# Attention followed by a low-rank token mixer and an MLP: where the third batch's attention begins, when a group's norms are issued, and the place of four small pieces of preparation

## The chip, the cores and the metric

The kernel runs on one core of a Trainium2 chip. The metric is the device time of one execution in microseconds. Before the change the median of three runs is 596.51 us (595.23 to 598.22). One more execution was profiled: 596.88 us, of which 595.1 us lie between the program's first and last instruction (the span).

## The reference, cut to what matters

```python
q, k, v: (8, 12, 448, 64)        # batch, heads, tokens, head size
q_n, k_n = rmsnorm(q, g_q), rmsnorm(k, g_k)
attn = softmax(q_n @ k_n.T / 8)
x = (attn @ v)                   # as (8, 448, 768)
h = x.transpose(0, 2, 1) @ U @ V # mixing over the tokens, rank 32
u = x + h.transpose(0, 2, 1)
out = u + relu(u @ w_ch1) @ w_ch2   # 768 -> 3072 -> 768
```

## The kernel before, in words

**Groups.** The 12 heads of a batch are worked in three groups of four; groups are numbered through all batches (group 3 is the first of the second batch, b = 1; group 6 the first of the third, b = 2). A group has two pairs of heads; a pair is named (b, pr).

**A group's preparation.** `load` (L125) puts its q, k and v into a set of three fp32 tiles (three sets take turns) by six DMAs on SP's queue. `squares` (L133) multiplies q and k with themselves, on ScalarE or GpSimd. `sums` (L159) adds up the squares on VectorE. `scale_all` (L203) issues `roots` (two small ScalarE instructions, L163), the scaling of q and k by them on GpSimd (L171, or L179 from group `DMA_FROM` = 6 on) and `values`, GpSimd's copies of v in bf16 (L197). Groups 1 to 5 are then turned by TensorE (`turn`, L347) and taken to SBUF by VectorE (`take_q`, `take_k`). From group 6 on four DMA transposes on SP's queue turn them (`turn_dma`, L373) and GpSimd multiplies the turned q with the gains (`take_dma`, L381). The scaled q (`qn`) and k (`kp`) have one buffer each, the turned ones (`qT`, `kT`) two.

**A pair.** `Sc` (L401) makes scores of 128 keys for both heads in one of two PSUM buffers and ScalarE takes their exponentials (L414). The last keys of both heads share one short block (`sl`). `Srows` issues two or three such blocks. `V` (L423) multiplies the exponentials with the values for half of the tokens; VectorE divides by the sum (L442) and writes `x` (L443).

**A batch's rest.** `mix_t` and `mix_tr` (L453, L462) project `x` to rank 32 and turn the result; `mix_rows` (L499), eight times, adds the mixed part to `x` on VectorE, and for each block of tokens an SP transpose writes `uT` (L521). `up` (L541: 24 times, six products each) makes the hidden layer, with the relu on ScalarE or VectorE; `down` (24 or 32 parts of six products, L552) the output, which VectorE adds to `x` (L569) and SP stores (L577). Batch 0 takes its own path through its mixing, with `prep_u` (L323), two casts of U, and `prep_v`, GpSimd's copies of V to `Vm`.

**Order.** No scheduler moves anything: each engine executes in the order in which the Python code issues. What comes first is an order written by hand (L605 to L641, and the calls from L752 on: there the loads of group 3's q and k stand ahead of group 2's v). Then two lists are merged: `att`, the attention of batches 1 to 7 and what prepares it (L643 to L718), and `mlp` (L729 to L750). Each entry has a cost in us. The loop at L820 takes the next entry of `att` as long as the cost taken so far is not above `due(cm)`, where `cm` is the cost taken from `mlp`; else it takes from `mlp`, where a batch's entries may begin once its attention is issued. `due` (L806) rises in one line up to the end of batch 1's attention while batch 0's MLP list runs, and in a second line over all that is left. An entry of cost 0 is issued where it stands. `load` is put off while a batch's `mix_rows` are being issued (`later`). `weights(n)` issues the next n pieces of the two weight matrices on GpSimd's queue.

In the merged order of before, around the change (groups in brackets):

```
up(0,21)  sums[6]  scale_all[6]  up(0,22)  Srows(1,4: two blocks)  turn_dma[6]  load[7]  take_dma[6]
weights(2)  V(1,3) x2  up(0,23)  Srows(1,4 and 1,5)  down(0,64) x2  V(1,4)  ...  V(1,4)  down
squares[7] on ScalarE  sums[7]  load[8]  V(1,5)  down  V(1,5)  down  Srows(2,0)  down x3  mix_t(1) ...
scale_all[7]  load[9]  Srows(2,0 and 2,1)  mix_rows(1) with down  ...  turn_dma[7]  take_dma[7]
```

Of the kernel before, what the change touches and what calls it, by code (L numbers as in the profile page):

```python
# [18 lines left out]
ROWS_FROM = 1  # L19
DMA_FROM = 6  # L20
LEAD = 1.8


@with_exitstack
def kernel(
# [13 lines left out]
    nc = tc.nc  # L39
# [3 lines left out]
    rank = moe_U.shape[1]  # L43
# [9 lines left out]
    NW = len(WIN[0])  # L53
# [19 lines left out]
    groups = []  # L73
# [16 lines left out]
    def load_qk(gi, i, eng=None):  # L90
        b, h0, n = groups[gi]
        if gi == BESIDE:
            for a in range(2):
                nc.sync.dma_start(staged[gi][i][a * R:(a + 1) * R].rearrange("p (c j) d -> p c (j d)", c=2),
                                  (q, k)[i][b, h0 + 2 * a:h0 + 2 * a + 2].rearrange("c (p j) d -> p c (j d)", j=NT))
            return
        src = (q, k)[i][b, h0:h0 + n].rearrange("(c a) (p j) d -> (a p) c (j d)", a=2, j=NT)
        (eng or nc.sync).dma_start(staged[gi][i].rearrange("p (c j) d -> p c (j d)", c=2), src)
# [4 lines left out]
    def load_v(gi, eng=None):  # L103
        b, h0, n = groups[gi]
        t = staged[gi][2]
        toks = v[b, h0:h0 + n].rearrange("h (p j) d -> p h (j d)", j=NT)
        for i in range(2):
            (eng or nc.sync).dma_start(
                t[i * R:(i + 1) * R, :NM, :].rearrange("p (h j) d -> p h (j d)", j=NJ),
                toks[:, :, i * NJ * D:(i + 1) * NJ * D])  # L110
        for e in range(2):
            hs = slice(e, 4, 2) if gi == BESIDE else slice(2 * e, 2 * e + 2)
            (eng or nc.sync).dma_start(t[e * R:(e + 1) * R, NM:, :], toks[:, hs, 2 * NJ * D:])

    def stage_tiles(gi):
        staged[gi] = [stage.tile([P, NM + 2, D], FP32, name=nm, tag=nm) for nm in ("qf", "kf", "vf")]
        ssqs[gi] = normp.tile([P, 2, NM + 2], FP32, name="ssq", tag="ssq")
        normed[gi] = [normp.tile([P, NT, 2, D], BF16, name="qn", tag="qn", bufs=1)]
        if gi < DMA_FROM:
            normed[gi].append(kp[:, :NT].rearrange("p j (c d) -> p j c d", c=2))  # L120
        else:
            normed[gi].append(kp)
        normed[gi] += [va_bufs[gi % 3], vl_bufs[gi % 3]]
# [167 lines left out]
    Ub = consts.tile([P, NJ + 2, rank], BF16)  # L291
    first = xp.tile([P, NW, dm], BF16, name="x", tag="x")
    Uf = first[:, 2, :2 * (NJ + 2) * rank].bitcast(FP32).rearrange("p (j r) -> p j r", r=rank)
# [3 lines left out]
    def load_u():  # L297
        for i in range(2):
            nc.sync.dma_start(Uf[i * R:(i + 1) * R, :NJ, :], Urows[:, i * NJ:(i + 1) * NJ, :])
        nc.sync.dma_start(Uf[R:P, NJ, :], Urows[:, 2 * NJ, :])  # L300
        nc.sync.dma_start(Uf[0:R, NJ + 1, :], Urows[:, 2 * NJ, :])
        nc.sync.dma_start(Vf, moe_V.rearrange("(m r) s -> m r s", m=1).to_broadcast([NQ, rank, S]))
# [17 lines left out]
    Uz = first[:, 0, :NW * P].rearrange("p (j r) -> p j r", r=P)  # L320
    tz = first[:, 1, :]

    def prep_u():  # L323
        nc.vector.tensor_copy(Ub, Uf)
        nc.vector.tensor_copy(Uz[:, :, :rank], Uf[:, :NW, :])

    tb_bufs = [consts.tile([P, 2 * P], BF16, name=f"tb{i}") for i in range(2)]

# [252 lines left out]
    att = []  # L581

    def add_att(cost, f, *a):
        att.append((cost, f, a))
# [17 lines left out]
    def turns(gi):  # L602
# [12 lines left out]
        (2, 1): scales(2) + [(0, weights, (1,)), V2(1, 0)],  # L615
        (2, 2): [(0, keep_busy, (6,))],
        (2, 3): [V2(1, 1), (0, prep_u, ())],
        (3, 0): [(0, keep_busy, (6,))],
        (3, 1): [V2(2, 0)],
# [23 lines left out]
    for i, (b, pr) in enumerate(pairs):  # L643
        if b == 0:
            continue
        gi, a = divmod(i, 2)
        more = gi + 1 < len(groups)
        by_dma = gi + 1 >= DMA_FROM
        soon = gi + 2 < len(groups)

        if a == 0:
            if pr == 0 and b > 1:
                add_att(0.5, V, *pairs[i - 1], 0)
                add_att(0.5, V, *pairs[i - 1], 1)
            add_att(0.45, Srows, ((b, pr, 0), (b, pr, 1)))
            if gi + 1 == DMA_FROM:
                add_att(0.0, turn_dma, gi + 1)
                add_att(0.0, load, gi + 2)
                add_att(0.0, take_dma, gi + 1)
                add_att(0.0, weights, 2)  # L660
            elif gi == DMA_FROM:
                add_att(0.0, scale_all, gi + 1)
                add_att(0.0, load, gi + 3)
            elif by_dma and more:
                add_att(0.0, scale_all, gi + 1)
            if b == 1 and pr == 0:
                add_att(0.8, lambda: None)
            if not by_dma:
                add_att(0.0, squares, gi + 1, 0, nc.gpsimd)
                add_att(0.0, squares, gi + 1, 1, nc.gpsimd)  # L670
                if gi + 2 < DMA_FROM:
                    add_att(0.0, load, gi + 3)
            if pr != 0:
                add_att(0.4, V, *pairs[i - 1], 0)
                add_att(0.5, V, *pairs[i - 1], 1)
            if not by_dma:
                add_att(0.0, sums, gi + 1, 0)
                add_att(0.0, sums, gi + 1, 1)
            add_att(1.0, Srows, ((b, pr, 2), (b, pr + 1, 0), (b, pr, 3)))
            if more and gi + 1 > DMA_FROM:  # L680
                add_att(0.0, turn_dma, gi + 1)
                add_att(0.0, take_dma, gi + 1)
                if gi > DMA_FROM and gi + 3 < len(groups):
                    add_att(0.0, load, gi + 3)
            if not by_dma:
                add_att(0.0, scale_all, gi + 1)
                if gi + 2 >= DMA_FROM:
                    add_att(0.0, squares, gi + 2, 0, nc.gpsimd)
                    add_att(0.0, squares, gi + 2, 1, nc.gpsimd)
            add_att(0.4, V, b, pr, 0)  # L690
        else:
            add_att(0.6, Srows, ((b, pr, 1), (b, pr, 2), (b, pr, 3)))
            if not by_dma:
                add_att(0.5, V, *pairs[i - 1], 1)
                add_att(0.39, T, gi + 1, 0)
                add_att(0.39, T, gi + 1, 1)
                if gi + 2 == DMA_FROM:
                    add_att(0.0, sums, gi + 2, 0)
                    add_att(0.0, sums, gi + 2, 1)
                    add_att(0.0, scale_all, gi + 2)  # L700
                continue
            if gi + 1 == DMA_FROM:
                add_att(0.5, V, *pairs[i - 1], 1)
                add_att(0.0, squares, gi + 2, 0)
                add_att(0.0, squares, gi + 2, 1)
                add_att(0.0, sums, gi + 2, 0)
                add_att(0.0, sums, gi + 2, 1)
                add_att(0.0, load, gi + 3)
                continue
            if soon:  # L710
                add_att(0.0, squares, gi + 2, 0)
                add_att(0.0, squares, gi + 2, 1)
            add_att(0.5, V, *pairs[i - 1], 1)
            if soon:
                add_att(0.0, sums, gi + 2, 0)
                add_att(0.0, sums, gi + 2, 1)
# [4 lines left out]
    done_at = {}  # L721
# [63 lines left out]
    sums(2, 0)  # L785
    stage_tiles(3)
    load_u()
    load_qk(3, 0)
    load_qk(3, 1)
    load_v(2)  # L790
    load_v(3)

    ia = im = 0
# [1 line left out]
    a_from = done_at[0]  # L795
    a_all = sum(c for c, _, _ in att[a_from:])
    a_one = sum(c for c, _, _ in att[a_from:done_at[1]])
    m_all = sum(m[0] for m in mlp)
    m_one = 0.0
    for m in mlp:  # L800
        if m[3] > 0:
            break
        m_one += m[0]
    m_end = m_all * (1.0 - LEAD / B)

    def due(c):  # L806

        if c < m_one:
            return a_one * min(1.0, c / (m_one - 3.0))
        return a_one + (a_all - a_one) * (c - m_one) / (m_end - m_one)  # L810

    def ready(f, a):
        if ca >= a_one:
# [6 lines left out]
    while ia < len(att) or im < len(mlp):  # L820
# [8 lines left out]
        if take_att:  # L829
            c, f, a = att[ia]  # L830
# [11 lines left out]
        else:  # L842
            c, f, a, _ = mlp[im]
# [34 lines left out]
```

## Time and profile before

| | us |
|---|---|
| median of three runs | 596.51 |
| profiled execution | 596.88 |
| its span | 595.1 |
| TensorE busy | 577.0 |
| ScalarE, GpSimd, VectorE busy | 303.1, 210.0, 198.9 |
| TensorE's pauses from 0 to 45 us | 7.7 |
| pauses from 75 to 87, 95 to 105, 105 to 121 us | 3.3, 1.1, 0.9 |
| mean granted TensorE clock of the span | 0.995 |

A row of the table by stage has the stage in us from the span's start, its length, the busy time (and number of instructions) of TensorE, its weight loads, VectorE, ScalarE and GpSimd, the granted clock of TensorE (1.00 is full), the busy share of the DMA engines and GB/s. A line of the waits has who waited, on which line, for whom, the sum in us, how often, and the longest. A line of a timeline has start, duration, engine, line, operation, tiles, shape, count, and in brackets the idle time ahead of it with what ended it. PE is TensorE, ACT ScalarE, DVE VectorE, POOL GpSimd, SP the queue from which most DMAs are issued.

### The profile page before, as it was taken

Reading aid. Unit: us, or ns where it says so; the run is one execution under the profiler, and the core shown is the slowest. Engines: PE = TensorE matmul, PEld = TensorE weight load, DVE = VectorE, ACT = ScalarE, POOL = GpSimd, SP = SyncE. Lnnn points to the kernel's source line nnn. Section 1 sums busy time; section 2 is a strip of 40 time slices with the busy share of each in tenths; the row PEclk is TensorE's granted clock in tenths of the full one; section 3 lists DMA queues with packets and bytes.
Section 4 is the critical chain, followed back from the end, with each engine's and each line's share of the span. In section 5 each row is a group of like instructions: output and inputs, shape, how many; then the busy total and the mean of one; then the engine's idle time right before and its main releaser. Section 6 shows DMA issues by size and latency. Waiting matters only on the chain.

```text
span 595.1 us, 11702 instructions
## 1 busy us (share of the span) xinstructions
PE 577.0 (97%) x4826; PEld 335.5 (56%) x4826; DVE 198.9 (33%) x459; ACT 303.1 (51%) x475; POOL 210.0 (35%) x308
## 2 busy tenths in 40 slices
PE   8889979999999999999999999999999999999996
PEld 7655545555556555655556554665556655655563
DVE  5865644512235213622225320541234310410011
ACT  6866744457635666447743577546753254014200
POOL 5975684354244152445053514424253000000000
PEclk9999989999999999999999999999999999999999
DMA  8899989874428560583345741658015210330022
GB/s 219 173 238 241 240 135 193 197 171 112 119 56 175 155 141 13 102 234 76 89 119 115 188 112 25 155 135 191 2 34 114 47 28 1 50 77 1 1 53 54
DMA packets 104509, 68.21 MB, mean 115 GB/s; under 512 B 66568, under 2 KB 101256, under 8 KB 104456
## 3 DMA queue, kind: packets, MB, share of 16 engines
q1 hardware_dynamic: 95044, 58.03, 41.7%
q0 software_dynamic: 9408, 9.44, 9.5%
q8 instruction: 38, 0.62, 0.4%
q14 instruction: 15, 0.12, 0.1%
q10 hardware_dynamic: 4, 0.00, 0.0%
HBM read 52.20 MB, written 11.01 MB: 106 GB/s over the span
## 4 chain that ended last, share of the span: by engine, by line
PE 82%; DMA 6%; POOL 3%; issue 3%; ACT 2%; SPq 2%; DVE 1%; POOLq 0%; ACTq 0%
PE po L559 34%; PE ph L527 33%; DMA vf<-in_v_dram 5%; PE pv L439 5%; PE sc L413 4%; PE sl L413 2%; PE pv L435 1%; PE pm L510 1%; POOL sq L141 1%; ACT E L414 1%; DMA kf<-in_k_dram 1%; SPq L521 1%; PE pu L458 1%; POOL kp L172 1%; DMA kT<-kp 1%
## 5 line engine op out<-in xcount | busy, mean ns | idle before, releaser
L559 PE MATMUL po<-w2b,hT 128*128 128x384 bf16 x1344 | 238.4, 327 | 0.0
L527 PE MATMUL ph<-uT,w1b 128*128 128x448 bf16 x1140 | 228.9, 352 | 0.1
L414 ACT ACTIVATE E<-sc,gg 128x896 bf16<-128x896 f32 (+1 forms) x150 | 140.4, 990 | 108.7 <-PE sc L413 108.3
L559 PEld LDWEIGHTS <-hT 128*128 128x128 bf16 x1344 | 126.2, 98 | 77.9 <-issue 4.8
L534 ACT ACTIVATE hT<-ph 128x448 bf16<-128x448 f32 x185 | 99.2, 549 | 127.7 <-PE ph L527 127.1
L527 PEld LDWEIGHTS <-w1b 128*128 128x128 bf16 x1140 | 108.2, 98 | 95.1 <-issue 2.4
L191 POOL TENSOR_TENSOR qn<-qf,rs 128x384 bf16<-128x384 f32 x36 | 29.9, 831 | 149.6 <-ACT rs L168 142.0
L442 DVE RECIPROCAL r<-pv 128x4 f32<-128x4 f32 x96 | 17.4, 181 | 189.2 <-PE pv L439 189.0
L384 POOL TENSOR_SCALAR qT<-qT,gg 128x448 bf16<-128x448 bf16 x36 | 50.6, 1405 | 70.8 <-DMA qT<-qn 59.8
L569 DVE TENSOR_TENSOR ob<-po,x 128x384 f32<-128x384 f32 x48 | 26.7, 557 | 104.1 <-PE po L559 103.3
L439 PE MATMUL pv<-va,E 128*128 128x65 bf16 x1152 | 57.1, 194 | 0.0
L439 PEld LDWEIGHTS <-E 128*128 128x128 bf16 x1152 | 50.5, 98 | 7.1 <-issue 0.9
L413 PE MATMUL sc<-qT,kT 64*128 64x448 bf16 (+1 forms) x294 | 43.8, 357 | 7.3 <-ACT E L414 5.4
L160 DVE TENSOR_REDUCE ssq<-sq 128x14 f32<-128x896 f32 x45 | 47.0, 1079 | 10.1 <-ACT sq L138 7.8
L435 PE MATMUL pv<-vl,E 128*128 128x130 bf16 x192 | 42.2, 220 | 1.1 <-POOL vl L201 0.9
L443 DVE TENSOR_TENSOR x<-pv,r 128x256 bf16<-128x256 f32 x96 | 40.7, 424 | 3.3
L413 PEld LDWEIGHTS <-kT 64*128 64x128 bf16 (+1 forms) x336 | 14.0, 94 | 46.2 <-issue 42.1
L515 DVE TENSOR_TENSOR x<-pm,x 128x384 bf16<-128x384 f32 x48 | 26.3, 554 | 17.9 <-PE pm L510 15.6
L191 POOL TENSOR_TENSOR kp<-kf,rs 128x384 bf16<-128x384 f32 x36 | 29.9, 830 | 0.0
L414 ACT ACTIVATE E<-sl,gg 128x448 bf16<-128x448 f32 x42 | 26.9, 641 | 0.0
L435 PEld LDWEIGHTS <-E 128*128 128x128 bf16 x192 | 18.7, 97 | 9.4 <-issue 2.5
L199 POOL CAST va<-vf 128x768 bf16<-128x768 f32 x24 | 19.8, 826 | 2.2 <-DMA vf<-in_v_dram 2.2
(93 smaller groups left out, 308.0 us busy)
## 6 DMA issues: line engine op xcount, KB each, us to landing
qf<-in_q_dram SPq DMA_DIRECT2D x23, 448.0 KB, 3.8
kf<-in_k_dram SPq DMA_DIRECT2D x23, 448.0 KB, 5.1
out_dram<-ob SPq DMA_DIRECT2D x50, 192.0 KB, 2.7
vf<-in_v_dram SPq DMA_DIRECT2D x48, 192.0 KB, 5.6
w1b<-in_moe_w_ch_dram POOLq DMA_DIRECT2D x4, 1152.0 KB, 18.2
w2b<-in_moe_w_ch_dram POOLq DMA_DIRECT2D x8, 576.0 KB, 14.9
vf<-in_v_dram SPq DMA_DIRECT2D x48, 32.0 KB, 4.8
out_dram<-ob SPq DMA_DIRECT2D x12, 96.0 KB, 4.2
```

The costliest lines, as they stand in the source:

```text
L160: nc.vector.tensor_reduce(ssqs[gi][:, i, :], sqs.pop((gi, i)), AX, ALU.add)
L191: nc.gpsimd.tensor_tensor(main.rearrange("p (t i) d -> p i t d", i=2), src[:, c, :2 * NJ].rearrange("p (i t) d -> p i t d", i=2), rs[:, c, ...
L384: nc.gpsimd.tensor_scalar(qT[:, a], qT[:, a], gg[:, 0:1], None, ALU.mult)
L413: nc.tensor.matmul(sc[:, i, :S], kT[d, keys], qT[d], start=True, stop=True)
L414: nc.scalar.activation(es[(b, pr)][:, 2 * r:2 * r + n, :], sc[:, :n, :S], AF.Exp, scale=scal, bias=bias)
L435: nc.tensor.matmul(pv[:, i].rearrange("p e d -> p (e d)"), E[:, 2 * NJ, w:w + P], vl[:, lp, :], start=True, stop=False)
L439: nc.tensor.matmul(pv[:, i, e, :], E[:, 2 * j + e, w:w + P], va[:, (first_h + step * e) * NJ + j, :], start=False, stop=(e == 1 and j == N ...
L443: nc.vector.tensor_tensor(xs[b].rearrange("p i (h d) -> p i h d", d=D)[:, 2 * half:2 * half + 2, h0:h0 + step + 1:step, :], pv[:, :, :, :D ...
L527: nc.tensor.matmul(ph, w1b[:, dt, ht * P:(ht + 1) * P], uT[:, dt, off:off + S], start=(dt == 0), stop=(dt == KD - 1))
L534: nc.scalar.activation(hT[:, ht, off:off + S], ph, AF.Relu)
L559: nc.tensor.matmul(po, hT[:, ht, col:col + P], w2b[:, ht, half * HALF:(half + 1) * HALF], start=(ht == 0), stop=(ht == KH - 1))
L569: nc.vector.tensor_tensor(ob[:, h], po, urows(b, col, half), ALU.add)
```

## The change

Six things are moved; none adds or leaves out arithmetic, and TensorE has the same products.

- `due` has three stretches instead of two: after batch 0's list the attention rests for 8.0 us of MLP cost, and then the third batch's attention is spread up to 53.0; the rest of the attention follows the old line within 1%. So Srows(2,0), which stood ahead of `mix_t(1)`, now stands after the last `mix_rows(1)`.
- Group 6's `sums` and `scale_all` move from behind `up(0,21)` to behind `up(0,23)`, around Srows(1,4 and 1,5); `turn_dma(6)`, `load(7)` and `take_dma(6)` follow V(1,4) instead of the first Srows(1,4).
- Group 7 is squared by GpSimd, behind `take_dma(6)`, instead of ScalarE; its `sums` move behind Srows(2,0).
- `load(8)` moves from ahead of V(1,5) to behind Srows(2,0); `load(9)` to behind `turn_dma(7)`.
- The last two weight pieces are issued behind GpSimd's squares of group 6 instead of behind `take_dma(6)`.
- In the start, `load_v(2)` goes ahead of group 3's q and k, and `prep_u`'s casts go from VectorE to GpSimd, where they stand ahead of `squares(3,0)`, which stands ahead of `values(2)` as before.

```diff
+REST = 8.0
+SECOND = 53.0
...
     def prep_u():
-        nc.vector.tensor_copy(Ub, Uf)
-        nc.vector.tensor_copy(Uz[:, :, :rank], Uf[:, :NW, :])
+        nc.gpsimd.tensor_copy(Ub, Uf)
+        nc.gpsimd.tensor_copy(Uz[:, :, :rank], Uf[:, :NW, :])
...
-            if gi + 1 == DMA_FROM:
-                add_att(0.0, turn_dma, gi + 1)
+            if gi == DMA_FROM:
+                add_att(0.0, sums, gi + 1, 0)
+                add_att(0.0, sums, gi + 1, 1)
                 add_att(0.0, load, gi + 2)
-                add_att(0.0, take_dma, gi + 1)
-                add_att(0.0, weights, 2)
-            elif gi == DMA_FROM:
-                add_att(0.0, scale_all, gi + 1)
-                add_att(0.0, load, gi + 3)
-            elif by_dma and more:
+            if by_dma and more and gi >= DMA_FROM:
                 add_att(0.0, scale_all, gi + 1)
...
-            if not by_dma:
+            if gi < DMA_FROM:
                 add_att(0.0, sums, gi + 1, 0)
                 add_att(0.0, sums, gi + 1, 1)
...
-                if gi > DMA_FROM and gi + 3 < len(groups):
+                if gi + 3 < len(groups):
                     add_att(0.0, load, gi + 3)
-            if not by_dma:
+            if gi < DMA_FROM:
                 add_att(0.0, scale_all, gi + 1)
...
+            if gi + 2 == DMA_FROM:
+                add_att(0.0, squares, gi + 2, 0, nc.gpsimd)
+                add_att(0.0, squares, gi + 2, 1, nc.gpsimd)
+                add_att(0.0, weights, 2)
...
-                if gi + 2 == DMA_FROM:
-                    add_att(0.0, sums, gi + 2, 0)
-                    add_att(0.0, sums, gi + 2, 1)
-                    add_att(0.0, scale_all, gi + 2)
                 continue
             if gi + 1 == DMA_FROM:
                 add_att(0.5, V, *pairs[i - 1], 1)
-                add_att(0.0, squares, gi + 2, 0)
-                add_att(0.0, squares, gi + 2, 1)
-                add_att(0.0, sums, gi + 2, 0)
-                add_att(0.0, sums, gi + 2, 1)
-                add_att(0.0, load, gi + 3)
+                add_att(0.0, turn_dma, gi + 1)
+                add_att(0.0, load, gi + 2)
+                add_att(0.0, take_dma, gi + 1)
+                add_att(0.0, squares, gi + 2, 0, nc.gpsimd)
+                add_att(0.0, squares, gi + 2, 1, nc.gpsimd)
                 continue
...
+    load_v(2)
     load_qk(3, 0)
     load_qk(3, 1)
-    load_v(2)
     load_v(3)
...
         if c < m_one:
-            return a_one * min(1.0, c / (m_one - 3.0))
-        return a_one + (a_all - a_one) * (c - m_one) / (m_end - m_one)
+            return min(a_one - 0.01, a_one * c / (m_one - 3.0))
+        c -= m_one
+        if c < REST:
+            return a_one - 0.01
+        if c < SECOND:
+            return a_one + (a_two - a_one) * (c - REST) / (SECOND - REST)
+        return a_two + (a_all - a_two) * (c - SECOND) / (m_end - m_one - SECOND)
```

## The prediction

> **What bounds the kernel now.** I read the sum of busy time first, then the table by stage, then the waits of TensorE, then the timelines around the longest.
>
> ```profile
> PE 577.0 (97%) x4826; PEld 335.5 (56%) x4826; DVE 198.9 (33%) x459; ACT 303.1 (51%) x475; POOL 210.0 (35%) x308
> ```
>
> ```profile
> 75.00:87.00 12.00, 8.70 (x72) 4.40 (x70) 5.79 (x16) 5.50 (x10) 10.07 (x15) 0.89 0.94 144
> 87.00:95.00 8.00, 8.00 (x82) 4.90 (x81) 1.70 (x5) 3.54 (x5) 6.18 (x9) 0.95 0.58 120
> 95.00:105.00 10.00, 8.89 (x89) 5.00 (x88) 4.82 (x10) 4.47 (x7) 2.99 (x6) 1.00 1.18 231
> 105.00:121.00 16.00, 15.13 (x133) 9.32 (x132) 8.21 (x16) 7.92 (x10) 5.24 (x8) 1.00 0.77 179
> ```
>
> TensorE is the bound: 577.0 of 595.1 us. From 121 us to the last products it never pauses, so nothing can be won there. What can be won is its pauses: about 8 us in the start (0 to 45 us), and those of the four rows above, where columns two and three are the stage and TensorE's busy time, and the third from the end is the granted clock. The waits from 20 to 130 us name them:
>
> ```profile
> PE sc L413 <- ACT E L414: 5.4, 6, 3.0
> PE pu L458 <- DVE x L443: 1.1, 1, 1.1
> PE pv L435 <- POOL vl L201: 0.9, 1, 0.9
> PE sc L413 <- DMA kT<-kp: 0.9, 1, 0.9
> PE ph L483 <- POOL Vm L317: 0.7, 1, 0.7
> PE sc L413 <- DVE kT L367: 0.4, 1, 0.4
> ```
>
> The 3.0 us one is at 81.55. The timelines of three engines show its cause:
>
> ```profile
> 79.73 1.67 POOL L141 TENSOR_TENSOR sq<-kf 128x896 f32<-128x896 f32 x1
> ...
> 81.43 1.08 DVE L160 TENSOR_REDUCE ssq<-sq 128x14 f32<-128x896 f32 x1 [0.55 <-POOL sq L141]
> ...
> 82.55 0.32 ACT L167 ACTIVATE rs<-ssq,eps 128x28 f32<-128x28 f32 x1 [4.26 <-DVE ssq L160]
> ```
>
> ScalarE is in order. Group 6's `roots` stand in its queue ahead of the exponentials of pair (1,4), and wait for GpSimd's squares and VectorE's sums; the exponentials hold both score buffers, and TensorE stands still until 84.51.
>
> **Removed between 81 and 122 us.** I count TensorE's work from 81.40 to 121.98 (both ends read from its timeline): 24 `down` parts at 0.976, four score steps of three blocks at 0.68, two of two blocks at 0.49, seven `V` at 0.49, `mix_t` and `mix_tr` 0.82, eight `mix_rows` at 0.165, in all 32.7 us. It took 40.6. Of the 7.9 us lost, these have names:
> - 2.96 and 0.34 at 81.55 and 85.07, the wait just shown;
> - the clock behind it: (1 - 0.89) x 12 + (1 - 0.95) x 8 = 1.7;
> - 1.11 at 100.28: `mix_t(1)` waits for the last `x`, which stands on VectorE behind group 7's sums, and these behind ScalarE's squares, which waited for load(7) (ScalarE idle 1.85 and 2.54 ahead of them);
> - 0.87 at 117.95: group 7's `kT`, whose transposes stand on SP behind two loads, outputs and batch 1's `uT`.
>
> Together 7.0. The other 0.9 I leave out.
>
> **What the change puts in their place.** From the order of instructions I follow after's queues by hand, with the durations above and before's clock up to 78.8.
>
> Step 1, group 6. GpSimd squares it as before, until 81.4, then issues the last two `w2` pieces (1.73, now ahead of the norm instead of behind `take_dma`), until 83.1. VectorE sums until 82.5. ScalarE now has first the exponentials of (1,4): two from 79.1 to 81.0, hT of `up(0,23)` to 81.9, two more to 83.7, one short to 84.25; then `roots`, which wait for nothing. TensorE: scores 81.40 to 82.1, two `down` parts to 84.0, then V(1,4,0), which needs the short exponential: **0.3 us** new. Then GpSimd's eight scalings and the values (5.67, as from 83.20 to 88.87) run 84.8 to 90.5. SP is past the two outputs of `down(0,64)` at 89.3, and issues four transposes at 1.25 until 94.4. Both queries are scaled on GpSimd at 95.9 (2.5 us to landing). Their first reader, Srows(2,0), now comes at 102.8. Hidden with 7 us.
>
> Step 2, load(7) and GpSimd's squares of group 7. The load goes out at 94.4. Before, q took 3.8 and k 6.7 with two `w2` pieces and load(8) beside it; at 121 us, without them, k took 4.6. So k lands between 99.6 and 101.7; I take 99.6, as the `w2` pieces now go 11 us sooner. The second square ends 1.68 later, at 101.3 (at the latest 103.4). Queued behind them on GpSimd: group 7's scaling, which needs the roots anyway. VectorE's sums stand behind `mix_rows`, not ahead of the last `x`: 103.4 to 105.5; roots 106.0; exponentials of (2,0) until 108.4. V(2,0,0) comes at 109.8: 1.4 us spare. `mix_t(1)` comes at 94.8, its `x` is done at 91.8. No pause.
>
> The row for a square is 1.68 on GpSimd and 0.95 on ScalarE, 1.46 more for the pair. [...]
>
> Step 3, SP behind it. A transfer waits until the eighth before it has landed (at 109.86 the first `uT` transpose started when the v piece issued at 100.71 landed). So `uT` starts when v(7) lands, 102.0 (issued 95.7, 6.3 as at 121.9), ends at 107.0 and lands 2.4 later; `up(1,0)` comes at 113.0. Then two outputs, load(8) at 108.2, two outputs, transposes of group 7 from 113.2. `kT` lands at 117.5, `qT` is scaled at 117.2, and Srows(2,2) comes at 118.0. Only 0.5 spare; I charge **0.3**.
>
> So 7.0 - 0.3 - 0.3 = 6.4 us.
>
> **The start.** TensorE waits 0.37 at 28.38 (for `kT`), 0.94 at 33.70 (for the third group's values) and 0.65 at 36.19 (for `Vm`, next on GpSimd): 2.0 in all.
>
> ```profile
> 25.40 1.68 POOL L172 TENSOR_TENSOR kp<-kf,rs 128x896 bf16<-128x896 f32 x1
> ...
> 34.29 0.30 POOL L201 CAST vl<-vf 64x128 bf16<-64x128 f32 x1 [1.04 <-DMA vf<-in_v_dram]
> ...
> 25.45 1.71 DVE L325 CAST x<-x 128x128 bf16<-128x128 f32 x1
> ```
>
> `prep_u`'s casts take VectorE 1.27 and 1.71 us and end 0.08 to 0.10 after GpSimd's scalings end. On GpSimd their price isn't in the trace: casts there take 0.29 (64x128) and 0.87 (32x384), so the two cost 0.6 to 1.7; by elements (160 and 128) I take 0.7. They run 27.9 to 28.6, before a 2.2 us idle time. [...]
>
> On GpSimd `squares(3,0)` stands ahead of `values(2)`. The v of group 2 goes out 1 us sooner and lands sooner, but q of group 3 now goes out at 21.6 instead of 19.0, behind it. Its landing is unknown: 26.8 (as before) to 34.2 (as the last of the six). The values end 1.69 + 1.5 later: 31.8 to 37.4, before 34.59. The gain is the difference, at most 2.0: **+2.0 to -2.8**. q has behind it k, which had 1.6 us of the old six; the weights' transfers begin at 26.4 and slow it; I take q at 30.1, values at 33.3, gain **1.3**. From 45 us on TensorE has no pause until 81.5, and what feeds it there follows GpSimd's own chain, which starts 1.3 sooner, so the gain is kept.
>
> **Sum.** 6.4 + 1.3 = 7.7 us. The profiled execution took 596.88 (span 595.1): 589.2. It lies 0.37 above the median 596.51: **588.8**.
>
> **Rivals.**
> - *The start backfires.* q of group 3 lands last, at 34.2, and GpSimd holds `values(2)` for it: 6.4 - 2.8 = 3.6, 592.9. For it: weights and loads share the transfers, share 1.16 from 25 to 35 us. Against: v, q and the small pieces ahead are 1.1 MB at the 0.2 MB per us of that stage. 0.12.
> - *SP takes the place of ScalarE.* Load(8) stands ahead of group 7's transposes. If transfers land as slowly as before's load(8) (q 8.6, k 10.1) and v(7) takes 8.2, `kT` lands at 123.3, 5.3 late, and the clock falls again (1.7): 7.7 - 7.0 = 0.7, 595.8, no change. For it: SP worked without rest from 85 to 128 us. Against: that slowness came with two loads and two weight pieces back to back; now one load at a time. 0.10.
> - *Slower.* GpSimd's squares of group 7 hold the norm: each us that k(7) lands behind 101.0 is a us of pause at V(2,0,0). Landing 7.7 later the gain is gone, and 599.5 needs 111.7, 17 us from issue. The k issued at 42.04 took 20.3, with weights beside it (share 1.13). At 94 us the weights are through; share 0.58. 0.03.
> - *Nothing is moved.* The order shows the sums behind `up(0,23)`; below 0.01.
>
> **How the numbers follow.** Forecast 0.75, 586.6 to 591.5: the low end is 7.9 + 2.0 = 9.9 gained, the high end 5.0. The range takes in the first rival: 586.6 to 593.0. About 0.5% (3 us) is what a measurement can tell: below 593.5 faster, 0.86; within, the second rival and part of the others, 0.10; slower 0.04.
>
> **What would show it.** After: no pause near 80 us and the granted clock 1.00 from 75 to 95; `mix_t(1)` near 93.5 with no wait; `up(1,0)` near 112 instead of 121.98; short waits at V(1,4,0) and Srows(2,2). In the start, `vl` of group 2 done near 33.3. I am wrong if L413 waits for `kT` over 1 us, if L435 waits for `vl` longer than 0.9, or if ScalarE idles before L167.

## The result, and the profile after

The changed kernel takes **589.96 us** (median of six runs, 589.48 to 592.45); the kernel before, beside it on the same chip, 595.03 (median of six, 594.00 to 598.22). The ratio is 0.9911, with a 95% interval from 0.9889 to 0.9933: 5.3 us gained (4.0 to 6.6), where the sum said 7.7. The time lies inside the range. The profiled execution of after took 590.86 (span 589.0), against 596.88 before.

In after, most lines have a number two higher (L413 is L415, L435 is L437, L384 is L386, L527 is L529). Its busy times are within 2% of before's:

```profile
PE 575.1 (98%) x4825; PEld 335.0 (57%) x4826; DVE 197.1 (33%) x458; ACT 300.2 (51%) x472; POOL 213.8 (36%) x312
```

The table by stage of after, in the columns of before's:

```profile
75.00:87.00 12.00, 11.77 (x119) 6.46 (x117) 5.97 (x17) 7.91 (x12) 9.98 (x14) 1.00 1.30 200
87.00:95.00 8.00, 8.00 (x98) 5.48 (x95) 2.94 (x9) 0.69 (x2) 4.16 (x7) 1.00 0.85 152
95.00:105.00 10.00, 10.00 (x81) 5.95 (x80) 7.37 (x13) 2.35 (x4) 4.28 (x3) 1.00 0.77 207
105.00:121.00 16.00, 13.99 (x104) 7.68 (x103) 4.41 (x8) 9.52 (x15) 7.39 (x13) 1.00 0.71 170
```

From 75 to 105 us TensorE is busy throughout but for 0.23 us, and the clock (third from the end) is 1.00 in every row. But the last row now lacks 2.01 us of 16, where before lacked 0.87. All waits of TensorE from 20 to 130 us in after:

```profile
PE sc L415 <- ACT E L416: 2.1, 4, 0.9
PE sc L415 <- POOL qT L386: 2.0, 1, 2.0
PE pt L354 <- POOL kp L174: 0.4, 1, 0.4
PE pv L437 <- ACT E L416: 0.2, 1, 0.2
```

The 3.0 us wait for the exponentials, the waits for `x`, `vl`, `Vm` and both for `kT` are gone. The 0.2 is V(1,4,0). The 0.4 for `kp` is at 20.0 us; before had 0.23 of it just ahead of this window. The 2.0 is new: Srows(2,2) at 117.38 waits for the turned and scaled q of group 7. The timeline of ScalarE in after shows the step that the change is named for:

```profile
80.81 1.90 ACT L416 ACTIVATE E<-sc,gg 128x896 bf16<-128x896 f32 x2
82.59 0.64 ACT L416 ACTIVATE E<-sl,gg 128x448 bf16<-128x448 f32 x1
83.11 0.33 ACT L169 ACTIVATE rs<-ssq,eps 128x28 f32<-128x28 f32 x1
```

`roots` (L169) now stands behind the exponentials of (1,4) and starts the moment they end. No bracket follows it: ScalarE did not idle ahead of it, where it had idled 4.26 us before.

### The profile page after: what moved, and what is told of

Same layout as the page of the kernel before. It is cut to its first block, busy times and chain, and to the rows that moved or that the text cites. A ratio compares the mean times of both kernels' runs of the same rounds, so it can differ in the third digit from the quotient of the medians.

```text
span 589.0 us, 11701 instructions
## 1 busy us (share of the span) xinstructions
PE 575.1 (98%) x4825; PEld 335.0 (57%) x4826; DVE 197.1 (33%) x458; ACT 300.2 (51%) x472; POOL 213.8 (36%) x312
## 4 chain that ended last, share of the span: by engine, by line
PE 91%; DMA 3%; SPq 1%; POOL 1%; ACT 1%; issue 1%; DVE 1%; POOLq 0%; ACTq 0%
PE po L561 36%; PE ph L529 36%; PE pv L441 6%; PE sc L415 5%; PE sl L415 2%; PE pv L437 2%; DMA qf<-in_q_dram 2%; PE pm L512 2%; ACT E L416 1%; DMA vf<-in_v_dram 1%; PE pu L460 1%; DMA qT<-qn 1%; PE pt L354 1%; POOL kp L174 1%; SPq L100 0%
## 5 line engine op out<-in xcount | busy, mean ns | idle before, releaser
L529 PE MATMUL ph<-uT,w1b 128*128 128x448 bf16 x1140 | 229.4, 352 | 0.0
L529 PEld LDWEIGHTS <-w1b 128*128 128x128 bf16 x1140 | 107.9, 98 | 95.1 <-issue 3.0
L386 POOL TENSOR_SCALAR qT<-qT,gg 128x448 bf16<-128x448 bf16 x36 | 50.5, 1402 | 73.1 <-DMA qT<-qn 54.3
L415 PE MATMUL sc<-qT,kT 64*128 64x448 bf16 (+1 forms) x294 | 43.3, 354 | 5.9 <-ACT E L416 3.0
L437 PE MATMUL pv<-vl,E 128*128 128x130 bf16 x192 | 42.2, 220 | 0.3 <-ACT E L416 0.2
L415 PEld LDWEIGHTS <-kT 64*128 64x128 bf16 (+1 forms) x336 | 14.1, 94 | 44.4 <-issue 38.2
L437 PEld LDWEIGHTS <-E 128*128 128x128 bf16 x192 | 18.7, 97 | 9.8 <-issue 2.0
L571 DVE TENSOR_TENSOR ob<-po,u_rest 128x384 f32<-128x384 f32 x8 | 4.5, 558 | 46.9 <-PE po L561 46.9
```

Source lines behind the costliest of these rows:

```text
L386: nc.gpsimd.tensor_scalar(qT[:, a], qT[:, a], gg[:, 0:1], None, ALU.mult)
L415: nc.tensor.matmul(sc[:, i, :S], kT[d, keys], qT[d], start=True, stop=True)
L437: nc.tensor.matmul(pv[:, i].rearrange("p e d -> p (e d)"), E[:, 2 * NJ, w:w + P], vl[:, lp, :], start=True, stop=False)
L529: nc.tensor.matmul(ph, w1b[:, dt, ht * P:(ht + 1) * P], uT[:, dt, off:off + S], start=(dt == 0), stop=(dt == KD - 1))
L571: nc.vector.tensor_tensor(ob[:, h], po, urows(b, col, half), ALU.add)
```

## The experiments

Ten kernels ran. Ratios are to the kernel before on the same chip (595.8 to 596.5 us there).

**1. After, with before's start.** The two casts of `prep_u` on VectorE, `load_v(2)` behind group 3's q and k:

```diff
-        nc.gpsimd.tensor_copy(Ub, Uf)
-        nc.gpsimd.tensor_copy(Uz[:, :, :rank], Uf[:, :NW, :])
+        nc.vector.tensor_copy(Ub, Uf)
+        nc.vector.tensor_copy(Uz[:, :, :rank], Uf[:, :NW, :])
...
-    load_v(2)
     load_qk(3, 0)
     load_qk(3, 1)
+    load_v(2)
```

> The kernel after with the old start: prep_u's casts back on VectorE, group 2's v loaded behind group 3's q and k. My theory (the start is worth 2.2 us, as the two profiles say when they are laid on each other at the same products): 2.2 us slower than after, about 3 us faster than before; the waits at L437 for vl (0.9) and for Vm (0.7) are back. Rival (the start gains nothing, since two runs differ there by a us anyway): the same as after, 5 us faster than before.

Measured: 591.97, ratio 0.9935 [0.9917, 0.9954], 3.9 us gained (2.7 to 4.9). Its profile has no wait for `vl` or `Vm` at all, though its start is before's; of the start's three waits only `kT`'s 0.4 is there. And it has the new pause, 2.5 us long:

```profile
PE sc L415 <- POOL qT L386: 2.5, 1, 2.5
...
PE sc L415 <- DVE kT L369: 0.4, 1, 0.4
```

Behind that pause the clock is at 0.50 for 3.41 us (119.42 to 122.83). So the middle alone gives less than the 6.4 of the sum: the pause takes 2.2 more than the 0.3 charged, and the fallen clock 1.7, which would leave 4.2 where the clock holds and 2.5 where it falls. Three of the six timed executions, this one among them, have a mean granted clock of 0.995, the others 0.997 to 1.000. And two of the three waits that the start was to remove are not in every execution of that start; I had expected both back.

**2. Before, with after's start alone** (the same lines, the other way round).

> The kernel before with the new start alone. My theory: 2.0 to 2.2 us faster than before; no waits at the first pv of group 2 for vl and at ph for Vm; the 3.0 us wait near 80 us stays. Rival (nothing in the start counts, TensorE's later waits are set by DMA landings): no change.

Measured: 595.07, ratio 0.9991 [0.9980, 1.0002]: 0.5 us gained, from a loss of 0.1 to a gain of 1.2. The expected 2.0 to 2.2 did not come.

**3 and 4. Its two halves in before:** only the casts on GpSimd, and only `load_v(2)` sooner.

> The kernel before with prep_u's casts on GpSimd alone. My theory (VectorE's casts wait for GpSimd, but what holds TensorE in the start is v's landing at 34.2): the casts take 0.3 us each on GpSimd, the wait for kT at 28.4 goes, the wait for vl grows by as much, total within 0.3 us of before. Rival (the casts held the whole start): 2 us faster.

> The kernel before with group 2's v loaded sooner alone. My theory: vl is done near 32, the waits for vl and Vm go, 1.6 us faster than before, the wait for kT stays 0.4. Rival from the prediction (q of group 3 lands last and GpSimd holds the values for it): vl done near 37, 2 to 3 us slower.

Measured: casts alone 1.0002 [0.9979, 1.0025], v alone 1.0004 [0.9987, 1.0022]: neither can be told from no change. The profiles do show the parts. With the casts alone the wait for `kT` is gone and `Vm`'s 0.6 stays; with v alone `vl` and `Vm` are gone and `kT`'s 0.4 stays. The gain on the whole time is too small to measure; the 1.6 us that I expected of v alone is not there.

**5. After, with group 7 squared by ScalarE:**

```diff
-                add_att(0.0, squares, gi + 2, 0, nc.gpsimd)
-                add_att(0.0, squares, gi + 2, 1, nc.gpsimd)
+                add_att(0.0, squares, gi + 2, 0)
+                add_att(0.0, squares, gi + 2, 1)
```

> The kernel after with group 7 squared by ScalarE instead of GpSimd, at the same place. My theory (what helps is that the sums stand behind the mixing; the engine of the squares has spare time): within 0.5 us of after; the sums of group 7 stand as in after. Rival (GpSimd's square of 1.68 is what holds group 7's norm and its qT, and a square of 0.95 on ScalarE shortens that): the 2.0 us wait at Srows(2,2) is shorter, 1 us faster than after. Third (ScalarE waiting for k of group 7 holds what is behind it): slower.

Measured: 591.33, ratio 0.9910 [0.9891, 0.9928] (after: 0.9911). The two can't be told apart (0.1 us, with an uncertainty of 1.7), so which engine makes these squares makes no difference that was measured.

**6. Before, with group 6's norm and turning a step later, and nothing else** (group 7's squares, its sums ahead of batch 1's last `x`, load(8) and `due` as before):

```diff
-            if gi + 1 == DMA_FROM:
-                add_att(0.0, turn_dma, gi + 1)
-                add_att(0.0, load, gi + 2)
-                add_att(0.0, take_dma, gi + 1)
-                add_att(0.0, weights, 2)
-            elif gi == DMA_FROM:
+            if gi == DMA_FROM:
...
-            if not by_dma:
+            if gi < DMA_FROM:
                 add_att(0.0, sums, gi + 1, 0)
                 add_att(0.0, sums, gi + 1, 1)
...
-            if not by_dma:
+            if gi < DMA_FROM:
                 add_att(0.0, scale_all, gi + 1)
...
-                if gi + 2 == DMA_FROM:
-                    add_att(0.0, sums, gi + 2, 0)
-                    add_att(0.0, sums, gi + 2, 1)
-                    add_att(0.0, scale_all, gi + 2)
...
+                add_att(0.0, turn_dma, gi + 1)
+                add_att(0.0, load, gi + 2)
+                add_att(0.0, take_dma, gi + 1)
+                add_att(0.0, weights, 2)
```

> The kernel before with only group 6's norm moved a step later (with its transposes, load(7) and gains, and the last weight pieces behind them), all else as before: group 7 squared by ScalarE and summed ahead of the last x of batch 1, load(8) there, the old order of batch 2. My theory (the parts hang together): the 3.0 us wait near 81 us goes, but load(7) goes out 3 us later in the program's work, and the sums of group 7 hold the last x: mix_t(1) waits 6 to 8 us instead of 1.1, and the clock falls there: 0 to 4 us slower than before. Rival (the parts add): 4 to 5 us faster than before.

Measured: 597.98, ratio 1.0026 [1.0013, 1.0039]: 1.5 us **slower** than before. Its waits of TensorE and two rows of its table by stage:

```profile
PE pu L458 <- DVE x L443: 5.1, 1, 5.1
...
PE sc L413 <- POOL qT L384: 1.7, 1, 1.7
```

```profile
87.00:95.00 8.00, 6.26 (x62) 3.91 (x61) 0.02 (x1) 0.00 (x0) 4.80 (x7) 1.00 0.54 96
95.00:105.00 10.00, 4.85 (x42) 2.64 (x40) 4.28 (x9) 4.13 (x6) 4.78 (x9) 0.66 1.12 255
```

The pause at 80 us is gone, as in after. But `turn_dma(6)` and load(7) go out later, and two waits grow out of that: the scores of (2,0), still ahead of the mixing, wait for group 6's q (1.7), and `mix_t(1)` waits 5.1 us (6 to 8 expected), not 1.1, for the last `x`, which stands on VectorE behind group 7's sums. The clock then falls to 0.66 in the row from 95 to 105.

**7. After, with before's two-line `due`:**

```diff
-            return min(a_one - 0.01, a_one * c / (m_one - 3.0))
-        c -= m_one
-        if c < REST:
-            return a_one - 0.01
-        if c < SECOND:
-            return a_one + (a_two - a_one) * (c - REST) / (SECOND - REST)
-        return a_two + (a_all - a_two) * (c - SECOND) / (m_end - m_one - SECOND)
+            return a_one * min(1.0, c / (m_one - 3.0))
+        return a_one + (a_all - a_one) * (c - m_one) / (m_end - m_one)
```

> The kernel after with the old due in two lines, so that batch 2's attention begins ahead of the second batch's mixing. My theory: Srows(2,0) comes near 92 and must wait for group 6's qT, scaled at 96 on GpSimd, so TensorE stands 3 to 5 us: 3 to 7 us slower than after. Rival (the rest of 8 us costs as much as it hides): the same as after.

Measured: 598.37, ratio 1.0038 [1.0020, 1.0055]: 2.3 us slower than before, and 7.6 slower than after by the two ratios, a little more than the 3 to 7 expected. Its longest waits:

```profile
PE sc L415 <- POOL qT L386: 3.8, 1, 3.8
PE ph L529 <- DVE ob L571: 2.2, 1, 2.2
```

The scores of (2,0) stand ahead of the mixing again and wait 3.8 us for group 6's q, whose transposes now go out behind V(1,4). Behind the first wait the clock is at 0.50 for 6.83 us (92.56 to 99.39). The later norm needs the later attention: both kernels that have the first without the second are slower than before. The later attention without the later norm was not run.

**8. After, with load(8) split:** `load_first` issues q and k where they were, `load_v` follows `turn_dma(7)` and `take_dma(7)`.

```diff
-                add_att(0.0, load, gi + 2)
+                add_att(0.0, load_first, gi + 2)
...
+                if gi == DMA_FROM:
+                    add_att(0.0, load_v, gi + 2)
```

> The kernel after with load(8) in two: q and k where they are, the four pieces of v behind group 7's transposes. My theory (Srows(2,2) waits 2.0 us for qT because SP issues load(8) ahead of the transposes): the transposes begin 2 to 2.5 us sooner, the wait of 2.0 goes below 0.3, 1.5 to 2 us faster than after. Rival (the first transpose waits for q of group 8 to land, not for SP): the transposes begin as before and the time stays as after's.

Measured: **587.68**, ratio 0.9858 [0.9836, 0.9880]: 8.5 us faster than before, and faster than experiment 5 (0.9910), which ran beside it and equals after. No pause over 0.23 us is left from 40 us to the end. SP's timeline in after, and then here, shows what moved (lines behind L132 have a number five higher here):

```profile
108.79 0.58 SPq L100 DMA_DIRECT2D qf<-in_q_dram  x1
109.42 0.49 SPq L100 DMA_DIRECT2D kf<-in_k_dram  x1
109.95 1.40 SPq L110 DMA_DIRECT2D vf<-in_v_dram  x2
111.40 1.26 SPq L115 DMA_DIRECT2D vf<-in_v_dram  x2
112.76 1.19 SPq L579 DMA_DIRECT2D out_dram<-ob  x2
114.06 2.32 SPq L378 DMA_TRANSPOSE qT<-qn  x1
116.47 1.21 SPq L380 DMA_TRANSPOSE kT<-kp  x1
```

```profile
106.76 0.58 SPq L100 DMA_DIRECT2D qf<-in_q_dram  x1
107.39 0.49 SPq L100 DMA_DIRECT2D kf<-in_k_dram  x1
107.98 1.13 SPq L584 DMA_DIRECT2D out_dram<-ob  x2
109.22 1.30 SPq L383 DMA_TRANSPOSE qT<-qn  x1
```

GpSimd's scaling of the turned q, first in after, then here (its start is the landing of the transpose, as the bracket says):

```profile
117.94 1.40 POOL L386 TENSOR_SCALAR qT<-qT,gg 128x448 bf16<-128x448 bf16 x1 [7.21 <-DMA qT<-qn]
```

```profile
113.81 1.40 POOL L391 TENSOR_SCALAR qT<-qT,gg 128x448 bf16<-128x448 bf16 x1 [4.63 <-DMA qT<-qn]
```

In after, k(8) landed at 114.07, the last v pieces seen at 115.78, the two outputs at 117.54, and the transpose 0.4 later. Here k(8) landed at 112.40, the outputs at 113.19, the transpose 0.4 later. So in both the transpose came in 0.4 behind what was issued before it on SP's queue, and in after v(8), 448 KB, was part of that. The transposes also go out sooner, because SP has not first to issue v(8)'s four pieces; the run doesn't tell the two effects apart.

**9 and 10. The split kernel with before's start, and with after's start once more, side by side.**

> This is the kernel with load(8) split, but with before's start (the casts of prep_u on VectorE, the v of group 2 behind the q and k of group 3). Beside it on the same chip the split kernel with the new start runs once more. If the start is worth the 1.3 us of the prediction in every execution, this kernel's median lies 1.3 above the other's (about 589.0 against 587.7). If the start's waits in the profile of before belong to that execution's landing times, the two lie within 0.5 of each other. In both cases the profile shows no wait for qT of group 7 near 117 us, and no window of half clock behind it.

> The kernel with load(8) split and the changed kernel's start, once more, as the partner of the one with before's start: about 587.7, 8 us below the kernel before, with no pause of TensorE over 0.5 us from 75 to 125 us.

Measured: 587.72, ratio 0.9869 [0.9849, 0.9889], with before's start; 588.59, 0.9866 [0.9845, 0.9887], with after's. The start makes 0.2 us, with an uncertainty of 1.7. Group 2's values in the profile with *before's* start, on GpSimd:

```profile
28.87 0.83 POOL L206 CAST va<-vf 128x768 bf16<-128x768 f32 x1
29.63 0.64 POOL L208 CAST vl<-vf 64x128 bf16<-64x128 f32 x2
```

No brackets: v had landed. In the profile of before the same three casts idled 2.18, 0.32 and 1.04 for it and ended at 34.59; here they end at 30.27.

My expectation for the last kernel missed in one point: its profile still has a pause at 117.34, though none over 0.5 us was expected.

```profile
PE sc L420 <- POOL qT L391: 1.5, 1, 1.5
```

There k(8) landed 5.3 us after its issue began (5.0 in experiment 8), and the transpose landed 1.9 behind the outputs and not 0.4. Why the transfers took longer there isn't settled. The split makes the pause rarer or shorter; it doesn't exclude it. The granted clock is 0.997 to 1.000 in all 14 executions of experiments 8, 9 and 10, and 0.995 in the slowest of after's six.

## Why the prediction was right in sign, and 2.4 us too large

**The mechanism in the middle was right.** Step by step, the predicted time and then that of after's trace (whose TensorE at 48 us ran 1.2 ahead of before's): group 6's sums end 82.5, 81.96; the values 90.5, 89.33; its transposes 94.4, 94.44; k(7) lands 99.6, 99.83; `uT` 102.0 to 107.0, 102.24 to 107.46; load(8) 108.2, 108.79; `mix_t(1)` 93.5, 93.84; `up(1,0)` near 112, 112.18. All but the last two are predicted on before's clock, and these two have the 1.3 of the start taken off. With 1.2 added to after's times, TensorE came within 0.4 of the steps (`mix_t(1)` 95.0 for 94.8, `up(1,0)` 113.4 for 113.0), but SP fell behind them: group 6's transposes end 95.6 for 94.4, load(8) goes out 110.0 for 108.2. So that SP's times agree as they stand is in part luck: the prediction had the start's lead reach everything behind it, and SP didn't keep it. In after, `uT` started when SP had issued the outputs ahead of it (102.14); the second piece of v(7) had landed by 101.50. The pause at V(1,4,0), charged 0.3, took 0.23. The clock loss is gone in the profiled execution: before had one stretch of 3.41 us at 0.50 (84.42 to 87.83), after has none between 6 and 580 us.

**The term that failed is the 0.3 charged for group 7's turned q and k at Srows(2,2).** It measured 2.0. The prediction had qT scaled at 117.2 and needed at 118.0, 0.8 of spare for q; both ends moved. SP reached the transposes at 114.06, not 113.2 (0.86). They landed 3.9 after issue, not 2.5: I took the median of 2.5 that before's transposes show, while here the six transfers of load(8) and two outputs stood ahead (1.3). And TensorE, 0.6 ahead, needed them at 117.38. That is 0.8 - 0.86 - 1.3 - 0.6 = -2.0, the pause. (On before's clock it is SP 2.1 late, the landing 1.3 late, and TensorE 0.6 late.) This is the rival "SP takes the place of ScalarE" in a small size: its mechanism happened, its price of 5.3 did not. My sentence on what would show me wrong named `kT`; `qT`, from the same four transposes, was the later of the two, since GpSimd still has 1.40 to do on it. Experiments 8 to 10 show that the order on SP is the cause: with v(8) behind the transposes the pause is gone in two profiles of three, and the ratio falls: 0.9911 and 0.9910 unsplit, 0.9858 and 0.9866 split; with before's start 0.9935 unsplit, 0.9869 split. With before's start and the split, experiment 9, the middle alone is worth 7.8 us (6.6 to 9.0). That takes in the 7.0 of named losses and the 7.9 with the part that had no name; the interval doesn't tell them apart.

**The start, 1.3, was a term of one execution.** The mechanism was right: in after the casts took 0.33 and 0.30 on GpSimd (I took 0.7 for both), group 2's values were done at 32.50 (predicted 33.3), and the three waits are gone.

```profile
28.95 0.33 POOL L326 CAST Ub<-x 128x160 bf16<-128x160 f32 x1
29.21 0.30 POOL L327 CAST x<-x 128x128 bf16<-128x128 f32 x1
29.47 1.68 POOL L143 TENSOR_TENSOR sq<-qf 128x896 f32<-128x896 f32 x1
31.10 0.82 POOL L201 CAST va<-vf 128x768 bf16<-128x768 f32 x1
```

Between the two profiled executions TensorE gains 2.2 us from 27 to 38 us (after stands 1.0 behind at the first and 1.2 ahead at the second). But 1.6 of the 2.0 us of waits came from v landing late, and the old order of loads doesn't always bring that: of its profiles, before has the waits for `vl` and `Vm`, experiment 3 has `Vm`'s alone, and experiments 1, 6 and 9 have neither. What is there each time with the casts on VectorE is `kT`'s 0.4. Timed, the start gave 0.5 (-0.1 to 1.2) in experiment 2, 1.4 with an uncertainty of 1.7 between after and experiment 1, and 0.2 with 1.7 between 9 and 10. So it is worth about half a microsecond, as far as was measured, and not 1.3. The sum with both terms corrected: 7.7 - 1.7 - 0.8 = 5.2, against 5.3 measured. What was measured is only known to lie between 4.0 and 6.6, so the agreement shows that these two terms suffice, not that they are exact.

**GpSimd's squares** were rightly costed at nothing, as far as experiment 5 can tell. The median square took 0.96 us on ScalarE and 1.67 to 1.68 on GpSimd, in before and in after alike. Why the longer duration cost no time is in after's trace: the squares end at 101.64, and `sums` stands on VectorE behind the last `x` and an output's addition, and begins at 102.42.

**VectorE's casts** took 1.27 and 1.71 beside GpSimd's scalings in before and in experiment 9, and ended 0.08 to 0.10 behind them; the same casts took 0.33 and 0.30 on GpSimd in after and in experiments 2 and 3, where `kT`'s wait of 0.4 is gone. No run had these casts on VectorE with GpSimd idle. So whether they waited for GpSimd, as I supposed for experiment 3, or took that long by themselves isn't shown.

**Not tried:** load(8) wholly behind group 7's transposes.

## What to carry to other kernels

A transfer on SP's queue landed behind all that was issued ahead of it there: cost it from the landing of the last transfer ahead (group 7's first transpose came 0.4 to 0.5 us behind it in five profiles, 1.9 in one), not from its issue alone, and put bulk loads with slack behind the small transfers that TensorE waits for. A wait for a first load that one profile shows may belong to that execution alone; look whether it follows from the order of work or from when a transfer happened to land. When a norm moves later, ask what was placed by its old time: here the attention that reads it and the loads behind it had to move along, and half of the edit was slower than none.

## What the runs showed of the hardware

**The clock fell at pauses of 2.52 us and more, and at none of 2.23 or less.** Every half-speed stretch between 6 and 580 us lasted 3.41 us or twice that (6.83), at 0.50. They began inside a pause or up to 1.7 us behind it: pauses of 2.96 (before), 2.94 (experiments 2 and 3), 2.95 (experiment 4), 2.52 (experiment 1), 3.81 (experiment 7) and 5.15 (experiment 6), the longer stretch in 3, 6 and 7. Pauses of 2.23 (experiment 5), 2.19 (a second one in experiment 7), 2.01 (after) and 1.53 (experiment 10) brought none.

Each stretch begins a whole number of 3.413 us (22 to 33 of them; 23 in before) after the trace's first reading of the clock. So I divided the traces into windows of this length, from that reading on. In the window just ahead of a stretch TensorE was idle for 2.14 us (experiment 7) to 2.95 (experiment 4), 2.87 in before; the windows at full clock that none followed had 1.60 or less, 1.46 at most in after. Two windows of experiment 1 and then two of experiment 5, divided in this way, show both cases (the stage, its length, and TensorE's busy time come first, the clock is third from the end):

```profile
116.00:119.42 3.42, 0.96 (x7) 0.50 (x8) 0.73 (x1) 1.02 (x2) 2.41 (x2) 1.00 0.62 99
119.42:122.83 3.41, 3.41 (x23) 1.88 (x22) 0.61 (x2) 2.38 (x5) 1.12 (x2) 0.50 0.95 322
```

```profile
114.71:118.13 3.42, 2.77 (x27) 1.42 (x24) 2.55 (x4) 3.26 (x6) 0.00 (x0) 1.00 0.52 113
118.13:121.54 3.41, 1.83 (x16) 1.00 (x17) 0.13 (x1) 1.37 (x2) 2.60 (x2) 1.00 0.57 91
```

The pause of 2.52 lay almost whole in one window (2.46); that of 2.23 was cut in two, as after's 2.01 was (1.46 and 0.56). A stretch of 3.41 at 0.50 costs 1.7 us. Whether the length of the pause decides, or the idle time of such a window, isn't shown: both part the cases, at 2.52 against 2.23 and at 2.14 against 1.60. Of the six timed executions of experiment 1, three have a granted clock of 0.995 and three of 0.997 to 1.000; only one of them was traced.

**SP's transfers landed in the order of issue, and none started before the eighth ahead of it had landed.** In all twelve profiles the landings that the trace records (197 of SP's 313 transfers in each) come in the order of issue, and no transfer starts before the eighth ahead of it has landed (192 such pairs in each). The second is how the program is built, as its instructions show: SP's transfers take eight semaphores in turn, and wait for their own (a wait that the traces record at 153 of the 313 in before and 155 in after). That the queue itself has such a limit is not shown.

**One of group 7's four transposes was slow to issue in five profiles of twelve.** In each of the profiles of after and of experiments 5, 8, 9 and 10 one of group 7's four transposes holds SP for 2.2 to 2.3 us, the others 1.2 to 1.5: the first in after (the row at 114.06), the second in experiment 5, the fourth in 8, 9 and 10. In experiment 1 the second took 1.64. In all six, load(8) (or its q and k) and two outputs stand just ahead on SP; in before and experiments 2, 3, 4, 6 and 7 three transposes of `uT` stand there, and none of the four takes over 1.26. What the slow one waits for is not shown.
